# Moving batch 1's kv and query turns behind one more output slot, with a later num 0, reordered w_out casts and one division moved to ScalarE

## The chip, the cores and the metric

One core of one Trainium2 chip. The metric is the device time of one execution, in us. Most executions agree within 0.5%, so ratios are given with their 95% intervals.

## The reference

Linear attention with cosine-weighted features, then a gated feed-forward layer. With r = relu(q) or relu(k), and c, s the cosine and sine of the position:

```python
q_p = concat(r_q * c, r_q * s);  k_p = concat(r_k * c, r_k * s)
kv  = einsum('bhsf,bhsd->bhfd', k_p, v);   z = sum_s(k_p)
x   = (q_p @ kv) / (q_p @ z + 1e-6)          # 8 batches x 8 heads, 576 positions, 64 wide
h   = x @ w_in                               # 4608 x 512 @ 512 x 2048
out = (h * sigmoid(beta * h)) @ w_out        # 2048 x 512, float32
```

## The kernel before

The tokens go through the feed-forward layer in nine chunks of 512. A chunk has 32 slots: 16 of h (four matmuls of 512 columns each), 16 of o (likewise). TensorE runs the slots back to back, and attention work of later batches is woven in between. Chunk 0 is special: batch 1's attention has to be woven into it while the loads of batch 1 and of the weights are still coming in. In the text, a turn is a transpose by TensorE, a take copies it out of PSUM, num 0 and num 1 are the products of q with kv for the two halves of the heads (the prediction's pair 0 and pair 1), and issue time is counted from start to start of the matmuls, since their recorded durations overlap (a matmul of 512 columns at L365 is recorded with 379 ns, and the next one starts 216 ns after it).

```python
def kv_take(jps, bank, eng="dve"):       # copies kv out of PSUM, banks 6 and 7
    ...
def q_turn_pe(b, jp, bank, hold=False):  # nine transposes of q into two banks; take() copies them out
    ...
def second():
    takes.append(q_turn_pe(1, 1, 6, hold=True))     # second query turn, into kv's banks
    cast_out(8)                                     # VectorE, w_out block 8
    takes[0]("act", 0); takes[0]("dve", 1)
    cast_out(9, "a")                                # ScalarE
    takes[0]("dve", 0); takes[0]("act", 1)
    cast_out(10)
    ...                                             # takes[1], blocks 11 to 15

early = {                                           # run behind the slot of that number in chunk 0
    4: lambda: (num_mm(8, 0, 2, 0), num_mm(8, 1, 2, 1), rest()),
    15: lambda: v_scale(1, 1, eng="act"),
    22: lambda: (kv_mm(1, 0, 6), kv_mm(1, 1, 6), kv_take((0, 1), 6, "act"),
                 takes.append(q_turn_pe(1, 0, 4, hold=True))),      # first query turn
    23: second,
    24: lambda: (num_seven(0, 4), x_mul(x_rden(4, 0, 0, 7, (0,)), 0, 7)),   # num 0 and its division
    26: lambda: (num_seven(1, 6), x_mul(x_rden(6, 0, 0, 7, (1,)), 0, 7)),   # num 1 and its division
    28: lambda: x_turn_pe(1, 0, 7, 4, ("act",), (0,)),
    29: lambda: x_turn_pe(1, 0, 7, 5, ("dve",), (1,)),
}
def rest():                                         # loads, in the order of the one load queue
    ...
    load_w("out", 0); load_w("out", 1)
    load_raw(1, "v"); load_raw(1, "k"); load_raw(1, "q")
    x_turn_dma(0, 8, 9)                             # transposing DMA, block 8 of batch 0
    load_w("out", 2, 2); load_w("out", 3, 2)
    ...
```

The lines that the profiles name: L108 casts w_in, L116 (VectorE) and L114 (ScalarE) cast w_out, L189 is a relu on VectorE, L229 a query turn, L234 and L217 take it out, L259 kv, L269 its copy, L280 num, L302 a division, L339 a turn of x, L365 h, L390 o.

## Time and profile before

| | before |
|---|---|
| time, first three runs | 295.02 us (294.88 to 295.82) |
| span of the profiled run | 293.1 us |
| TensorE busy, granted clock | 282.5 us, 0.998 |
| kv of batch 1 starts | 37.98 us |
| q's relu starts (its load has landed) | 39.52 us |
| cast of w_out block 8 starts (likewise) | 41.35 us |
| chunk 1 starts on TensorE | 51.31 us |

The last four rows are starts in the timeline of TensorE and VectorE. The lines of the profile stand in the prediction.

### The profile page before, as it was taken

The numbers are of one execution on the slowest core, as the hardware profiler recorded it, in microseconds if no ns is written. First come the engines' busy times: TensorE is split into PE (matmuls) and PEld (weight loads), VectorE is DVE, ScalarE is ACT, GpSimd is POOL, SyncE is SP. The second block draws the span as 40 slices with busy tenths as digits, with TensorE's granted clock in tenths as the row PEclk, the third lists the DMA queues.
The fourth block names the chain that finished last, engine by engine and source line by source line (L and its number), as shares of the span: only waits on it lengthen the run. The fifth ranks groups of instructions, "written<-read, shape, count | busy, mean of one in ns | idle before, by whom it ended". The sixth has DMA issues, their size and how long they took to land.

```text
span 293.1 us, 7188 instructions
## 1 busy us (share of the span) xinstructions
PE 282.5 (96%) x3046; PEld 143.2 (49%) x3073; DVE 115.0 (39%) x292; ACT 142.5 (49%) x226; POOL 73.3 (25%) x85
## 2 busy tenths in 40 slices
PE   8699989999999999999999999999999999999994
PEld 7454455455445544454445544554455444444444
DVE  5999976743910292029400950087005000000000
ACT  5768756862157324821474137512760277137511
POOL 1440000642381028202640255015701210000000
PEclk9999999999999999999999999999999999999999
DMA  7999999999999079906991699139102910131033
GB/s 259 369 394 382 392 292 389 290 250 341 162 262 352 5 147 236 400 12 130 220 386 58 121 221 394 57 65 188 54 2 53 142 36 0 38 83 24 0 74 72
DMA packets 50737, 53.89 MB, mean 184 GB/s; under 512 B 31233, under 2 KB 31633, under 8 KB 50705
## 3 DMA queue, kind: packets, MB, share of 16 engines
q1 hardware_dynamic: 47744, 45.95, 53.5%
q0 software_dynamic: 2688, 7.34, 10.4%
q8 instruction: 24, 0.39, 0.6%
q10 hardware_dynamic: 272, 0.14, 0.2%
q14 instruction: 9, 0.07, 0.1%
HBM read 36.71 MB, written 9.44 MB: 157 GB/s over the span
## 4 chain that ended last, share of the span: by engine, by line
PE 84%; DMA 8%; DVE 3%; issue 1%; SPq 1%
PE ps L390 39%; PE ps L365 38%; DMA raw_q<-in_q_dram 5%; PE ps L280 3%; DMA raw_v<-in_v_dram 3%; PE ps L259 2%; DVE win L108 2%; PE ps L408 1%; SPq L78 1%; DVE xs L302 1%; PE ps L229 0%; DVE vb L204 0%; DVE rden L295 0%; PE ps L339 0%; DVE qb L189 0%
## 5 line engine op out<-in xcount | busy, mean ns | idle before, releaser
L365 PE MATMUL ps<-xt,win 128*128 128x512 bf16 (+1 forms) x580 | 127.4, 378 | 0.1
L390 PE MATMUL ps<-wout,g_t 128*128 128x512 bf16 x535 | 120.4, 379 | 2.1 <-issue 1.1
L372 ACT ACTIVATE g_t<-ps,beta 128x512 bf16<-128x512 f32 x144 | 98.5, 688 | 33.3 <-PE ps L365 33.3
L365 PEld LDWEIGHTS <-win 128*128 128x128 bf16 x580 | 56.0, 98 | 66.1 <-DVE win L108 0.7
L390 PEld LDWEIGHTS <-g_t 128*128 128x128 bf16 x560 | 53.9, 98 | 63.6
L385 POOL DMA_DIRECT2D out_dram<-o_sb x56 | 37.2, 668 | 144.9 <-ACT o_sb L396 144.9
L396 ACT COPY o_sb<-ps 128x512 f32<-128x512 f32 x35 | 20.2, 587 | 98.2 <-PE ps L390 94.0
L271 DVE CAST kv<-ps 128x520 bf16<-128x520 f32 x6 | 4.2, 699 | 68.3 <-PE ps L259 68.3
L217 POOL TENSOR_TENSOR qs<-qt,tanr 128x1152 bf16<-128x1152 bf16 x12 | 28.4, 2382 | 7.2 <-DMA qt<-qb 6.4
L411 DVE COPY o_sb<-ps 128x256 f32<-128x256 f32 (+1 forms) x2 | 0.7, 358 | 62.9 <-PE ps L408 62.9
L302 DVE TENSOR_TENSOR xs<-ps,rden 128x768 bf16<-128x768 f32 (+5 forms) x27 | 23.1, 862 | 0.9
L291 DVE TENSOR_TENSOR den<-ps,eps 128x12 f32<-128x12 f32 (+4 forms) x26 | 4.2, 160 | 33.6 <-PE ps L280 33.5
L214 DVE TENSOR_SCALAR vb<-raw_v,cos 128x256 bf16<-128x256 f32 x63 | 17.1, 347 | 0.0
L214 DVE TENSOR_SCALAR vb<-raw_v,sin 128x256 bf16<-128x256 f32 x54 | 14.7, 347 | 0.0
L280 PEld LDWEIGHTS <-qt 64*64 64x64 bf16 x576 | 10.5, 106 | 4.7 <-issue 3.4
L280 PE MATMUL ps<-kv,qt 64*64 64x65 bf16 x576 | 11.7, 195 | 0.5 <-ACT kv L269 0.5
L189 DVE TENSOR_SCALAR qb<-raw_q 128x1152 bf16<-128x1152 f32 x16 | 11.4, 752 | 1.6 <-DMA raw_q<-in_q_dram 1.6
L259 PE MATMUL ps<-vb,rk 64*64 64x130 bf16 x576 | 10.2, 218 | 1.7 <-ACT rk L187 1.6
L280 PE MATMUL ps<-kv,qs 64*64 64x65 bf16 x576 | 11.5, 193 | 0.0
L108 DVE CAST win<-w_stage 64x512 bf16<-64x512 f32 x26 | 11.2, 433 | 0.6
L259 PEld LDWEIGHTS <-rk 64*64 64x64 bf16 x576 | 8.5, 106 | 5.6 <-issue 2.5
L189 DVE TENSOR_SCALAR rk<-raw_k 128x2304 bf16<-128x2304 f32 (+2 forms) x9 | 10.5, 1172 | 0.6 <-DMA raw_k<-in_k_dram 0.6
(59 smaller groups left out, 98.5 us busy)
## 6 DMA issues: line engine op xcount, KB each, us to landing
raw_v<-in_v_dram SPq DMA_DIRECT2D x7, 1152.0 KB, 10.5
raw_k<-in_k_dram SPq DMA_DIRECT2D x7, 1152.0 KB, 13.2
raw_q<-in_q_dram SPq DMA_DIRECT2D x7, 1152.0 KB, 7.4
out_dram<-o_sb POOLq DMA_DIRECT2D x56, 128.0 KB, 4.0
w_stage<-in_moe_w_in_dram SPq DMA_DIRECT2D x3, 1024.0 KB, 13.6
w_stage<-in_moe_w_out_dram SPq DMA_DIRECT2D x2, 1024.0 KB, 8.8
w_stage<-in_moe_w_out_dram SPq DMA_DIRECT2D x4, 512.0 KB, 11.2
out_dram<-o_sb SPq DMA_DIRECT2D x14, 128.0 KB, 2.3
```

The source lines that it names most:

```text
L108: nc.vector.tensor_copy(o, a)
L189: nc.vector.tensor_scalar(dst, src, scalar1=0.0, scalar2=None, op0=ALU.max)
L214: nc.vector.tensor_scalar(o, a, scalar1=t[:, n : n + 1], scalar2=None, op0=ALU.mult)
L217: eng.tensor_tensor(dst.rearrange("q n (g p) -> q n g p", g=2), src.rearrange("q n (g p) -> q n g p", g=2), tanr[:, n0:n1].unsqueeze(2).to ...
L259: nc.tensor.matmul(t[jj * HP : (jj + 1) * HP, g], lhsT=rk[hs, n, 2 * jp + jj, :], rhs=vb[hs, n, 2 * jp + jj].rearrange("q s e -> q (s e)") ...
L280: nc.tensor.matmul(ps[cols, bank + jj, slot * E : (slot + 1) * E], lhsT=(qt, qs)[cs][rows, jp, n, cols], rhs=kv[rows, g, jp, cs, :], start ...
L302: nc.vector.tensor_tensor(o.rearrange("q j n s d -> q j (n s) d"), nv[:, :, a:z, :, 0:D].rearrange("q j n s d -> q j (n s) d"), rden[:, :, ...
L365: nc.tensor.matmul(ps[:, h_bank(c, jt), blocks.start * 64 : blocks.stop * 64], lhsT=win[jt // 4][:, mi, (jt % 4) * P : (jt % 4 + 1) * P], ...
L372: nc.scalar.activation(g_t, ps[:, h_bank(c, jt)], AF.Silu, scale=beta[:, jt : jt + 1])
L385: eng.dma_start(out=out_v[bb, n][:, m0:m1], in_=o_sb[hf * HP : (hf + 1) * HP, m0:m1])
L390: nc.tensor.matmul(o_ps, lhsT=gs[c, jt][:, tt * P : (tt + 1) * P], rhs=wout[jt // 4][:, jt % 4, :], start=(jt == 0), stop=(jt == JT - 1))
L396: nc.scalar.copy(o_sb, o_ps)
```

## The change

It means to fill an idle stretch of TensorE ahead of the first query turn with slot 23, whose weights are there long before, and then to keep the rest of the chain from being pushed.

```diff
-    x_mul(x_rden(6, 0, 7, 8, (1,)), 7, 8)              # stood behind the two x_mul
+    x_mul_act(x_rden(6, 0, 7, 8, (1,)), 7)             # now ahead of them
 def second():
+    kv_mm(1, 0, 6); kv_mm(1, 1, 6); kv_take((0, 1), 6, "act")
+    takes.append(q_turn_pe(1, 0, 4, hold=True))
     takes.append(q_turn_pe(1, 1, 6, hold=True))
     ...
-    cast_out(11, "a"); cast_out(12)
-    for j in range(13, JT):
+    for j in (11, 12, 14, 15):
         cast_out(j, "a")
 early = {
-    22: lambda: (kv_mm(1, 0, 6), kv_mm(1, 1, 6), kv_take((0, 1), 6, "act"),
-                 takes.append(q_turn_pe(1, 0, 4, hold=True))),
     23: second,
-    24: lambda: (num_seven(0, 4), x_mul(x_rden(4, 0, 0, 7, (0,)), 0, 7)),
+    25: lambda: (num_seven(0, 4), x_mul(x_rden(4, 0, 0, 7, (0,)), 0, 7), cast_out(13)),
```

More of the change, by code (lines that the diff above doesn't have):

```diff
@@ L534, in second @@
     def second():
+        kv_mm(1, 0, 6)
+        kv_mm(1, 1, 6)
+        kv_take((0, 1), 6, "act")
+        takes.append(q_turn_pe(1, 0, 4, hold=True))
         takes.append(q_turn_pe(1, 1, 6, hold=True))
@@ L545, in second @@
             takes[1](e, i)
-        cast_out(11, "a")
-        cast_out(12)
-        for j in range(13, JT):
+        for j in (11, 12, 14, 15):
             cast_out(j, "a")
```

## The prediction

> **What bounds the kernel now.** I read the totals first, then the chain that ended last, then TensorE's own order of work around the change. The totals say that TensorE is the engine to watch: it is busy 282.5 of 293.1 us, at a granted clock of 0.998.
>
> ```profile
> PE 282.5 (96%) x3046; PEld 143.2 (49%) x3073; DVE 115.0 (39%) x292; ACT 142.5 (49%) x226; POOL 73.3 (25%) x85
> ```
>
> So 10.6 us of the span have no matmul, and only those, and matmuls that could be left out, are to be had. The change leaves out no matmul. The chain of work that ended last, in order of time, shows where the rest is:
>
> ```profile
> 3.02 8.94 DMA raw_v<-in_v_dram
> ...
> 24.08 15.41 DMA raw_q<-in_q_dram
> 39.52 0.77 DVE qb L189
> 41.06 0.81 PE ps L390 x3
> ...
> 52.72 10.47 PE ps L365 x48
> ...
> 82.30 11.22 PE ps L365 x52
> ```
>
> The columns are start, length, and what. From 40.3 us on the chain is TensorE nearly without a break (the waits of TensorE after 53 us sum to 1.0 us in six pieces of up to 0.2, all labelled "issue"). Ahead of that it runs through a load: batch 1's q, issued at 24.08, lands at 39.49, and the relu of its first half (0.77 us) is what TensorE waits for. TensorE in order of time, before the stretch that changes and in it:
>
> ```profile
> 31.84 6.21 PE L390 MATMUL ps<-wout,g_t 128*128 128x512 bf16 x27
> 37.98 1.22 PE L259 MATMUL ps<-vb,rk 64*64 64x130 bf16 x72
> 40.33 0.68 PE L229 MATMUL ps<-ident,qb 128*128 128x128 bf16 x9 [1.13 <-DVE qb L189]
> 41.06 0.81 PE L390 MATMUL ps<-wout,g_t 128*128 128x512 bf16 x3
> 41.71 0.67 PE L229 MATMUL ps<-ident,qb 128*128 128x128 bf16 x9
> 42.21 1.03 PE L390 MATMUL ps<-wout,g_t 128*128 128x512 bf16 x4
> ```
>
> The bracket is idle time and its cause. Slots 16 to 22 of chunk 0 are 28 output matmuls (27 recorded), then kv of batch 1, then 1.13 us of nothing until q's relu is done. Behind it stand the four matmuls of slot 23 (three recorded), which need none of this: their weights were cast long before. This 1.13 us is the prize.
>
> VectorE and ScalarE in the same window say what else could hold TensorE once that gap is filled:
>
> ```profile
> 39.52 1.43 DVE L189 TENSOR_SCALAR qb<-raw_q 128x1152 bf16<-128x1152 f32 x2 [1.58 <-DMA raw_q<-in_q_dram]
> 41.35 0.48 DVE L116 TENSOR_SCALAR wout<-w_stage,rbeta 128x512 bf16<-128x512 f32 x1 [0.40 <-DMA w_stage<-in_moe_w_out_dram]
> 41.75 1.42 DVE L217 TENSOR_TENSOR qs<-ps,tanr 128x512 bf16<-128x512 bf16 x2
> 45.45 0.49 DVE L116 TENSOR_SCALAR wout<-w_stage,rbeta 128x512 bf16<-128x512 f32 x1 [0.56 <-DMA w_stage<-in_moe_w_out_dram]
> 46.33 1.09 DVE L302 TENSOR_TENSOR xs<-ps,rden 128x896 bf16<-128x896 f32 x1
> 47.81 1.09 DVE L302 TENSOR_TENSOR xs<-ps,rden 128x896 bf16<-128x896 f32 x1
> ```
>
> The relus of both halves of q are over only at 40.95. Block 8 of w_out lands at 41.33 and its cast ends at 41.83; slot 24 needs it. Block 12's cast waits 0.56 us for its own load and holds the division of pair 0 up behind it.
>
> [...]the chain's 52 matmuls in 11.22 us are 216 each[...], and four matmuls of a slot are 0.87 us.[...] For two scaled copies of 64 columns[...] the same operation on pair 0 took 0.50 us in the trace, which I use.[...] ScalarE waits four times, 1.6 us in all, for VectorE's qs before its qt.[...]
>
> **Part 1: kv and the query turns behind slot 23.** Nothing is removed; 4 x 216 = 0.87 us of matmuls go ahead of kv. From the trace, slot 22 ends its issue at 37.98, so kv starts at 37.98 + 0.87 = 38.85 (its last input, k's relu, ended at 37.93, so it is no longer even close), and 1.15 us later, its length on the chain in the steady batches, TensorE is free: 40.00. The first query turn still cannot start before 40.33. So the gap falls from about 1.2 us of issue time to 0.33: 0.87 gained at this point. But the next two things now come sooner than their inputs:
> - The first turn issues in 0.50 us (nine loads in 0.50), to 40.83. The second stood behind slot 23 and needed nothing; now it waits for the second half's relu: 40.95 plus 0.05 to wake, 41.00. Loss 0.17. Its bank 6 also waits for kv to be copied out: kv ends about 40.07, the copy takes 0.59 on ScalarE, 40.76; not the last.
> - The second turn issues to 41.50. Slot 24 needs block 8 of w_out, cast until 41.83 at the end of a load that does not move: 41.88. Loss 0.38. Before, slot 24 started at 42.21, so at this point the gain is 0.33.
>
> **Part 2: num 0 a slot on.** Before, num 0 started at 43.22 although slot 24 had issued by 42.21 + 0.87 = 43.08: it waited for the last qs of pair 0 (VectorE, until 43.17). That is 0.14 us. Now slot 25 comes first; slots 24 and 25 take 41.88 to 43.61, past 43.17, so the wait is gone: 0.14 gained. (The 0.16 "issue" gap after num 0 is where slot 25's first matmul is missing from the records; I count nothing for it.) Slot 25 needs block 9's cast on ScalarE, done at 42.13; slot 26 needs block 10, done by VectorE at 43.56, and starts about 44.2. Neither binds. Num 1 then starts about 45.1, after its takes (VectorE to 44.88, ScalarE to 44.77).
>
> **Part 3: w_out casts reordered.** Block 12 goes from VectorE to ScalarE, block 13 to VectorE behind the division of pair 0. ScalarE: block 11 to 45.39, block 12 from its landing at 45.41 to 46.17; slot 28 needs it at about 46.5. VectorE: the division of pair 0 starts at 44.90 instead of 45.85, takes 1.57 as before, ends 46.45; block 13 to 46.87 (slot 29 needs it at 47.8); the division of pair 1 ends about 48.4, and its turn stands at 48.6. This part gains nothing by itself; it keeps num 0's later place from pushing the second turn of x.
>
> From 41.88 on TensorE's work is eight slots, 32 x 216 = 6.92, two nums at 0.60 together 1.20, two x turns at 0.39: 8.90. Sum 50.78, against a chunk 1 that began at 51.31. **Gain 0.53 us**: 0.33 + 0.14, and 0.06 of rounding.
>
> **Part 4: block 7 of pair 1 on ScalarE.** VectorE loses a 0.29 us multiply but does this block's denominators first, so the seven other blocks' two multiplies end at about 18.5, not 18.23. The last transpose, now bound by these, goes from 18.88 to about 18.7, and VectorE's w_in casts begin 0.3 us sooner. ScalarE is idle from 17.0 to 18.26, so two copies (0.50) fit there. TensorE is some 0.2 us earlier through chunk 0's first half. But it meets a load: q lands at 39.49 whatever the engines do, since the DMA engines moved 385 to 395 GB/s in every window I asked for from 14 to 32 us and were still above 350 in the mean from 32 to 38; no earlier issue makes that shorter. The 0.2 us are handed back as a longer wait ahead of the first query turn. **Worth nothing** at the end.
>
> **Rivals.**
> - *The gap is gained whole.* 0.87 + 0.14, perhaps 0.2 more from part 4: 294.0 or just under. For it: TensorE bounds everything after, and moves over unhindered. Against: the relu at 40.95 and the cast at 41.83 are fixed by loads, and I see no way around the latter.
> - *The wait only moves.* Slot 24's weights, then VectorE's run from takes to divisions, hold TensorE until the old times: 295.0. For: VectorE is in the same order until 44.88, and the second division ends (48.4) only some 0.2 us before its turn. Against: before, the second turn of x had nothing to wait for at 49.19, with its division over at 48.90.
> - *A transfer shifts.* The stretch from 38 to 40 us has only 145 GB/s, while a transposing DMA and the rest of q land; if a little earlier work on VectorE changes the order in which the queue is fed, q or w_out could land half a microsecond sooner or later: 293.9 or 295.4. In the trace nothing on the queue of these loads hangs on what the change moves, so I give it little.
>
> **Range and chances.** 295.02 - 0.53 = 294.5. The three runs before lay from 294.88 to 295.82, so the spread of runs is as large as the gain. First rival and last set the low end, 293.9; the second and a slow median set the high end, 295.1. Two per cent is 5.9 us, eleven times the whole gap that can be filled and over half of all idle time of TensorE; neither side of 2% is reachable without a fault that I don't see.
>
> **What would show it.** Right: kv starts at about 38.85; the idle ahead of the first query turn falls from 1.13 to about 0.3; short new idles ahead of the second turn (q's relu) and slot 24 (a w_out cast); no wait ahead of num 0; chunk 1 begins about 50.8; identical lengths after it. Wrong: slot 24 starting before 41.8 or after 42.1 (the cast of block 8 is then not what binds); an idle ahead of the second x turn (VectorE's run binds); q landing elsewhere than 39.5 (the loads moved); part 4 seen in the start of chunk 1.

0.33 + 0.14 and 0.06 of rounding are 0.53 us, 295.02 - 0.53 is 294.5 us, and each length is one of the trace before (216 ns a matmul, from 52 in 11.22 us; "0.05 to wake": q's first relu ends at 40.27 us, the turn that waits for it starts at 40.33). In the trace the w_out casts on ScalarE have a median of 722 ns, and the division of one block of one pair (part 4's multiply) takes 0.29 us.

## The result, and the profile after

294.55 us (294.51 to 294.71, four runs) against 295.12 (294.88 to 295.82, four runs). The ratio is 0.9978, interval 0.996 to 0.9995; it is the mean time of one kernel's fast runs over that of the other's of the same rounds, so not quite the ratio of the medians. The predicted 294.5 was hit. Two later sessions on two chips, with six runs of the changed kernel in each, did not confirm the gain: 0.9997 and 0.9999 (below). So the number was right in its session, and the reason has to be looked at.

The totals after, from the page; TensorE has no matmul more or less:

```profile
PE 282.4 (96%) x3046; PEld 142.5 (49%) x3073; DVE 114.3 (39%) x291; ACT 142.6 (49%) x228; POOL 73.3 (25%) x85
```

The chain that ended last, after (start, length, what). It now hangs on w_in and w_out loads, no longer on q's; 45.31 shows a stop inside num 1 that nothing explains there:

```profile
6.29 12.66 DMA w_stage<-in_moe_w_in_dram
...
31.17 9.53 DMA w_stage<-in_moe_w_out_dram
...
41.22 0.65 PE ps L229 x9
...
45.13 0.18 PE ps L280 x6
45.31 0.14 issue
45.45 0.60 PE ps L280 x45
```

TensorE in order of time, after:

```profile
31.91 7.07 PE L390 MATMUL ps<-wout,g_t 128*128 128x512 bf16 x31
38.91 1.22 PE L259 MATMUL ps<-vb,rk 64*64 64x130 bf16 x72
40.06 0.68 PE L229 MATMUL ps<-ident,qb 128*128 128x128 bf16 x9
41.20 0.66 PE L229 MATMUL ps<-ident,qb 128*128 128x128 bf16 x9 [0.46 <-DVE wout L116]
41.70 1.89 PE L390 MATMUL ps<-wout,g_t 128*128 128x512 bf16 x7
```

kv starts at 38.91, as predicted, and the first turn follows without idle: the 1.13 us are gone. But the second turn now idles 0.46 us. The profile names a cast as the cause. A cast of weights is no input of a query turn, so the name is only that of the semaphore event that came last; in the second trace of this kernel the same wait is put down to the copy of kv (`<-ACT kv L269`), which empties the turn's bank. VectorE after:

```profile
38.89 1.43 DVE L189 TENSOR_SCALAR qb<-raw_q 128x1152 bf16<-128x1152 f32 x2 [1.63 <-DMA raw_q<-in_q_dram]
40.72 0.49 DVE L116 TENSOR_SCALAR wout<-w_stage,rbeta 128x512 bf16<-128x512 f32 x1 [0.40 <-DMA w_stage<-in_moe_w_out_dram]
41.12 1.48 DVE L217 TENSOR_TENSOR qs<-ps,tanr 128x512 bf16<-128x512 bf16 x2
...
44.71 1.09 DVE L302 TENSOR_TENSOR xs<-ps,rden 128x896 bf16<-128x896 f32 x1
45.72 0.48 DVE L116 TENSOR_SCALAR wout<-w_stage,rbeta 128x512 bf16<-128x512 f32 x1
...
46.66 1.09 DVE L302 TENSOR_TENSOR xs<-ps,rden 128x896 bf16<-128x896 f32 x1
```

Both loads came 0.63 us sooner than in the trace before (38.89 against 39.52, and 40.72 against 41.35), although the prediction held that nothing moves them. And ScalarE's copy of kv, before and then after:

```profile
39.31 0.59 ACT L269 CAST kv<-ps 128x520 bf16<-128x520 f32 x1 [1.98 <-PE ps L259]
```

```profile
40.56 0.59 ACT L269 CAST kv<-ps 128x520 bf16<-128x520 f32 x1 [3.89 <-PE ps L229]
```

Before, the copy starts 0.11 us after kv's last matmul (37.98 + 1.22 = 39.20). After, 0.43 us (38.91 + 1.22 = 40.13). The records of semaphore events have kv's at 40.16; ScalarE's wait instruction was over at 40.19; the copy that stands behind it started at 40.56 with nothing to wait for. So three questions: is the earlier landing the change's doing, what holds the copy of kv, and what is the change worth without both.

### The profile page after: what moved, and what is told of

It is laid out like the page before. It is cut to its first block, busy times and chain, and to the rows that moved or that the text cites. A ratio compares the mean times of both kernels' runs of the same rounds, so it can differ in the third digit from the quotient of the medians.

```text
span 292.9 us, 7188 instructions
## 1 busy us (share of the span) xinstructions
PE 282.4 (96%) x3046; PEld 142.5 (49%) x3073; DVE 114.3 (39%) x291; ACT 142.6 (49%) x228; POOL 73.3 (25%) x85
## 4 chain that ended last, share of the span: by engine, by line
PE 84%; DMA 9%; DVE 4%; issue 1%; SPq 0%
PE ps L390 39%; PE ps L365 38%; DMA w_stage<-in_moe_w_in_dram 4%; PE ps L280 3%; DVE win L108 3%; DMA w_stage<-in_moe_w_out_dram 3%; PE ps L259 2%; DMA raw_q<-in_q_dram 2%; PE ps L408 1%; DVE wout L116 0%; PE ps L339 0%; PE ps L229 0%; SPq L78 0%; DVE xs L302 0%; DVE o_sb L411 0%
## 5 line engine op out<-in xcount | busy, mean ns | idle before, releaser
L302 DVE TENSOR_TENSOR xs<-ps,rden 128x768 bf16<-128x768 f32 (+4 forms) x26 | 22.8, 884 | 1.0 <-DVE rden L295 0.2
L280 PEld LDWEIGHTS <-qs 64*64 64x64 bf16 x576 | 10.5, 105 | 0.2 <-issue 0.2
```

The costliest lines, as they stand in the source:

```text
L280: nc.tensor.matmul(ps[cols, bank + jj, slot * E : (slot + 1) * E], lhsT=(qt, qs)[cs][rows, jp, n, cols], rhs=kv[rows, g, jp, cs, :], start ...
L302: nc.vector.tensor_tensor(o.rearrange("q j n s d -> q j (n s) d"), nv[:, :, a:z, :, 0:D].rearrange("q j n s d -> q j (n s) d"), rden[:, :, ...
```

## The experiments

Each ran with a profile and, beside the kernel before on the same chip, for three or five rounds. All give correct results.

**First call: chance in the loads, and block 7 by itself.** The first two kernels are the two of the study, unchanged. `block7_only` is the kernel before with the first hunk of the diff alone, `block7_undone` the changed kernel without it.

```diff
 # block7_only: kernel before; block7_undone: changed kernel with - and + exchanged
+    x_mul_act(x_rden(6, 0, 7, 8, (1,)), 7)
     x_mul(got, 0, 4)
     x_mul(got, 4, 7)
-    x_mul(x_rden(6, 0, 7, 8, (1,)), 7, 8)
```

> The kernel before, unchanged: a second trace, to see how far the loads' landings vary by themselves. In the first trace batch 1's q landed at 39.49 us, in the trace after the change at 38.87, although the DMA engines had moved the same bytes by 22 and by 36 us. Theory A, the landing varies by chance[...]: q lands somewhere from 38.8 to 39.6 here, and the kernel takes 295.0. Theory B, the change moves the landing: 39.5 again here and in every run that leaves the change's first part out, 38.9 in every run that has it.

> The changed kernel, unchanged. Expected ratio to before 0.998, 294.5 us. ScalarE's copy of kv waits some 0.36 us after its semaphore was met in the first trace (wait over at 40.19, copy from 40.56). If that is bound to the instruction's place in ScalarE's stream, it is there again with the same size; if it was chance, it is gone and the second query turn starts about 0.3 us sooner after kv.

> The kernel before with block 7 of pair 1 on ScalarE and nothing else of the change. The prediction's step: worth nothing, 295.0, ratio 1.000 with 0.999 to 1.001, since q's landing takes the 0.2 us back. Rival: the loads are fed sooner (theory B) and the first query turn starts 0.6 us sooner: 294.4.

> The changed kernel with block 7 back on VectorE. ScalarE then has two instructions fewer ahead of the copy of kv. Prediction's step (worth nothing): 294.5, as the changed kernel. Theory of the place in the stream: the 0.36 us ahead of the copy of kv are gone, the copy starts under 0.1 us after its semaphore, the second turn follows the first with 0.1 us less idle or more, and the kernel is 0.1 to 0.4 us faster than the changed one: 294.2. Theory B of the loads: q lands at 39.5 and it is 0.1 slower.

Measured, median and ratio: before again 295.16 (0.9999), after again 294.98 (0.9997, interval 0.9978 to 1.0017), block7_only 295.24 (0.9997), block7_undone 295.34 (1.0011, 0.9987 to 1.0034). No time differs beyond its interval, and neither the 294.5 us expected of the changed kernel nor the 294.2 of block7_undone came. The traces do differ.

The landing of q varies from run to run. q's relu started at 39.52 in the first trace before and at 39.04 in the second; with block 7 on ScalarE at 38.89 and 38.95 (the changed kernel) and 39.47 (`block7_only`); with the change but without block 7 at 40.01. That is theory A; theory B (the change moves the landing) asked for two groups. The parts of one load land apart as well: in the first trace before, k's sixteen parts landed from 34.10 to 36.55 us. Over all eleven traces with the old load order q's relu started anywhere from 38.89 to 40.05. So comparing two single traces mixes the change with this. Part of the spread goes with how late the queue was fed. In six of the eleven, q's load was issued at 23.89 to 24.15 us and its last part landed at 38.87 to 39.49; in the other five, issued at 24.31 to 24.99, it landed at 39.45 to 40.03. What makes the landings differ at the same time of issue stays open.

The 0.36 us ahead of the copy of kv are not chance. They are 0.36 us in all three traces that have block 7's two instructions on ScalarE and 0.04 in all three that have not, also in the otherwise changed kernel, `block7_undone`. Its TensorE:

```profile
39.33 1.22 PE L259 MATMUL ps<-vb,rk 64*64 64x130 bf16 x72
40.82 1.34 PE L229 MATMUL ps<-ident,qb 128*128 128x128 bf16 x18 [0.28 <-DVE qb L189]
42.38 1.89 PE L390 MATMUL ps<-wout,g_t 128*128 128x512 bf16 x7 [0.21 <-DVE wout L116]
```

Both turns are one group here (x18), 0.28 us idle for q's relu ahead and 0.21 us behind for the cast of block 8: two of the waits that the prediction had named, in a run with a late load. The third stands inside the group, where the line doesn't show it: the second turn starts 0.21 us after the start of the first's last transpose, against 0.06 where nothing holds it (kv_at_22), so it waits 0.16 us for the relu of q's second half.

**The remaining parts, the place of the copy, and kv back at its slot.**

```diff
 # kv_at_22: changed kernel
-    kv_mm(1, 0, 6); kv_mm(1, 1, 6); kv_take((0, 1), 6, "act")     # out of second()
+    22: lambda: (kv_mm(1, 0, 6), kv_mm(1, 1, 6), kv_take((0, 1), 6, "act")),
 # act_shift: changed kernel
-    15: lambda: v_scale(1, 1, eng="act"),
+    15: lambda: (nc.scalar.copy(warm, zero_b), v_scale(1, 1, eng="act")),
 # num0_at_24: changed kernel
-    25: lambda: (num_seven(0, 4), x_mul(...), cast_out(13)),
+    24: lambda: (num_seven(0, 4), x_mul(...), cast_out(13)),
 # casts_old: changed kernel
-    for j in (11, 12, 14, 15): cast_out(j, "a")                   # and no cast_out(13) at slot 25
+    cast_out(11, "a"); cast_out(12)
+    for j in range(13, JT): cast_out(j, "a")
```

> The changed kernel with kv and its copy back behind slot 22; both query turns stay together behind slot 23. In the two traces of the changed kernel the second turn waits 0.47 us for the copy of kv, which empties its bank. Theory: with slot 23 (0.87 us) between kv and the turns this wait is gone; the second turn follows the first without idle, or waits for q's relu alone, and slot 24 starts when block 8's cast is over (landing of that w_out block + about 0.55 us). Slot 24 to start 0.4 us sooner than in the changed kernel at the same landings (41.2 to 41.3 where block 8 lands at 40.7), and the run to take 0.3 to 0.5 us less: ratio to before 0.9965 to 0.9985. Rival: VectorE's takes and divisions hold TensorE later on, and nothing is gained over the changed kernel.

> The changed kernel with one idle copy of one column added to ScalarE ahead of the scaling of batch 1's v, so that the copy of kv is the 65th and not the 64th of its recorded instructions. Theory of the place: the 0.36 us between met semaphore and copy are gone (under 0.1 us), the second turn starts 0.3 us sooner after kv, if q's relu is over by then. Rival (the copy waits for the transposes' writes, or for their semaphore): 0.36 us again. Worth 0.1 to 0.3 us at most.

> The changed kernel with num 0 back behind slot 24 (its place before), the casts as changed. Prediction's step: a wait of TensorE for the last qs of pair 0 ahead of num 0. With slot 24 at 41.6 and the qs over at 42.5 the wait is about 0.1 us by the traces; by the prediction 0.14 and more, since slot 24 comes sooner. So slower than the changed kernel by 0.1 to 0.3 us, or nothing where slot 24 came late. Rival: num 0 sooner makes the division sooner and something later gains: not slower.

> The changed kernel with the w_out casts in their old order (block 12 on VectorE ahead of the division of pair 0, 13 to 15 on ScalarE). Prediction's step: worth nothing by itself, but block 12's load then holds up the divisions: the first ends about 47.4 at a landing of 45.4, the second 1.5 us later, against x turns wanted at 47.4 and 48.7. So an idle of 0 to 0.3 us ahead of an x turn, and as much in the time; at the earlier landings of the last traces nothing.

Measured: kv_at_22 294.98 (0.999, 0.9971 to 1.0008), act_shift 295.24 (1.0, 0.9981 to 1.002), num0_at_24 295.21 (1.0007, 0.9988 to 1.0025), casts_old 294.74 (0.9991, 0.9972 to 1.0009). Again the times alone decide nothing; kv_at_22's lies above the range expected for it (0.9965 to 0.9985).

*act_shift.* TensorE, then ScalarE's copy:

```profile
39.20 1.22 PE L259 MATMUL ps<-vb,rk 64*64 64x130 bf16 x72
40.45 1.38 PE L229 MATMUL ps<-ident,qb 128*128 128x128 bf16 x18
42.48 1.89 PE L390 MATMUL ps<-wout,g_t 128*128 128x512 bf16 x8 [0.66 <-DVE wout L116]
```

```profile
40.52 0.59 ACT L269 CAST kv<-ps 128x520 bf16<-128x520 f32 x1 [3.06 <-PE ps L259]
```

The copy starts 0.10 us after kv (39.20 + 1.22 = 40.42), though the transposes follow as closely as before. So neither the transposes' writes nor their semaphore held it. One more or two fewer instructions ahead of it do away with the 0.36 us: the cost belongs to the place, the 64th recorded instruction of ScalarE (its waits counted). The second turn's wait shrinks with it but isn't gone: the x18 hides 0.20 us of it (0.26 us from the first turn's last start to the second's first, against 0.06), as the copy of kv ends at 41.11 and the relu of q's second half at 41.06. This run's w_out load was late (the cast began at 41.94), and slot 24 waited 0.66 us for it, so the time shows no gain.

*num0_at_24.* The wait ahead of num 0 is back, with 0.31 us where 0.1 to 0.3 was expected:

```profile
41.87 1.02 PE L390 MATMUL ps<-wout,g_t 128*128 128x512 bf16 x4
...
43.20 0.22 PE L280 MATMUL ps<-kv,qt 64*64 64x65 bf16 x4 [0.31 <-DVE qs L217]
```

Yet chunk 1 starts 13.13 us after slot 22's end, against 13.05 and 13.09 in the first two traces of the changed kernel: the stop inside num 1 (below) isn't there, and the one pays for the other (from slot 24 to chunk 1 it is 9.42 us here and 9.39 in the first trace of the changed kernel).

*casts_old.* Block 12's cast waits 0.60 us for its load on VectorE and pushes the second division to 48.61, but the turn of x that needs it starts at 49.01, without idle:

```profile
45.16 0.49 DVE L116 TENSOR_SCALAR wout<-w_stage,rbeta 128x512 bf16<-128x512 f32 x1 [0.60 <-DMA w_stage<-in_moe_w_out_dram]
...
47.52 1.09 DVE L302 TENSOR_TENSOR xs<-ps,rden 128x896 bf16<-128x896 f32 x1
```

```profile
49.01 0.55 PE L339 MATMUL ps<-ident,xs 128*128 128x128 bf16 x7
```

Chunk 1 starts 13.06 us after slot 22's end, as with the new order. The casts' order is worth nothing at this landing.

*kv_at_22.* kv, slot 23, both turns and slot 24 run without idle, although the copy of kv has its 0.38 us here too; it has slot 23's length to hide in:

```profile
39.23 1.22 PE L259 MATMUL ps<-vb,rk 64*64 64x130 bf16 x72
40.38 1.04 PE L390 MATMUL ps<-wout,g_t 128*128 128x512 bf16 x4
41.25 1.17 PE L229 MATMUL ps<-ident,qb 128*128 128x128 bf16 x18
42.26 1.89 PE L390 MATMUL ps<-wout,g_t 128*128 128x512 bf16 x8
```

Chunk 1 starts 12.08 us after slot 22's end. Of the 13.07 us of the changed kernel, 0.64 are the second turn's wait in issue time (from 40.06 + 0.50 to 41.20 in the first trace) and 0.35 the stop inside num 1; 12.08 + 0.64 + 0.35 = 13.07.

**The transposing DMA in the load queue, and the best version.** In the trace before, the window from 38 to 40 us, in which q ends and the transposing DMA runs, moved little. The line gives packets and mean rate:

```profile
DMA packets 213, 0.29 MB, mean 145 GB/s; under 512 B 83, under 2 KB 83, under 8 KB 213
```

```diff
 # before_turn8: kernel before; kv22_turn8: kv_at_22
-        x_turn_dma(0, 8, 9)                              # in rest()
+    9: lambda: x_turn_pe(0, 8, 9, 1, ("act",)),          # in early
```

> The kernel before, but block 8 of batch 0 is turned by TensorE behind slot 9 (two transposes, a copy of 256 columns by ScalarE) and not by a transposing DMA, which stood in the load queue between batch 1's q and w_out's third quarter. So far chunk 1 of the kernel before began 11.58 us after q's landing in both its load-bound traces, and q's sixteen parts all landed within 0.1 us, about 1.8 us behind the last bytes of the steady stream. Theory: the loads drain at that transposing DMA, and without it q lands 1 us or more sooner (about 38.0) and block 8 of w_out 1.5 us sooner; TensorE then waits for neither, chunk 1 begins 12.4 us after slot 22's end, some 0.3 to 1.0 us sooner than in the kernel before: ratio 0.997 to 0.999. Rival: q[...] lands near 39.3 as before; only w_out comes 0.46 us sooner, and the time is the same.

> The changed kernel with kv behind slot 22 and block 8 of batch 0 turned by TensorE, as the best that the runs point to. If the transposing DMA drains the loads: no wait of TensorE from slot 22 to chunk 1, which begins 12.3 us after slot 22's end whatever the landings; 294.2, ratio 0.996 to 0.998, and its runs spread less. Rival: q at 39.3; then no better than the run with kv behind slot 22 (0.999).

> The changed kernel a third time, to be timed on the same chip beside the two others. From its traces chunk 1 begins 13.1 to 13.2 us after slot 22's end, or 9.4 us after the landing of w_out's block 8, whichever is later; the kernel before needs 12.3 or 9.8. So about 0.35 us better where the load is late and up to 0.9 worse where it is early: near 1.000 in the mean, 0.998 to 1.001.

> The best version once more, on another chip. Its five runs took 294.01 in the median against 295.33, ratio 0.9953; but its trace, set against the kernel before at the same landings (chunk 1 of that begins 11.6 us after q's landing, so at 50.6 against 49.98), accounts for 0.6 us alone, 0.998. If its lead comes from the waits that it no longer has, the ratio lies between 0.996 and 0.998 here, and its interval stays under 1; if the first lead was luck with the loads of those runs, it is 0.998 to 1.000.

Measured: before_turn8 295.5 (1.0002, 0.9986 to 1.0019); kv22_turn8 294.01 (293.58 to 294.21), ratio **0.9953** (0.9935 to 0.997), and on another chip 293.95 (293.71 to 294.64), **0.9971** (0.9957 to 0.9985); after_third 295.37 (0.9999, 0.9983 to 1.0015).

The rival was right on q's landing. The same window of before_turn8 is full:

```profile
DMA packets 406, 0.78 MB, mean 388 GB/s; under 512 B 30, under 2 KB 30, under 8 KB 406
```

But q's relu starts at 39.94 there and the first turn waits 1.19 us. In the traces of both orders q's last part lands 2.9 to 3.0 us after k's last part, with or without the transposing DMA: so the DMA does not set that distance; what does was not shown. What the DMA cost was behind q: block 8's load now lands 1.37 us after q's instead of 1.82. The kernel before does not wait for that block, so it gains nothing. kv22_turn8 needs the block sooner, and has no wait left in its first trace:

```profile
38.12 1.22 PE L259 MATMUL ps<-vb,rk 64*64 64x130 bf16 x72
39.26 1.04 PE L390 MATMUL ps<-wout,g_t 128*128 128x512 bf16 x4
40.14 1.17 PE L229 MATMUL ps<-ident,qb 128*128 128x128 bf16 x18
41.14 1.89 PE L390 MATMUL ps<-wout,g_t 128*128 128x512 bf16 x8
...
50.19 1.03 PE L365 MATMUL ps<-xt,win 128*128 128x512 bf16 x4
```

In its second trace q's relu came at 39.40, and the two turns lost 0.3 us to it (chunk 1 starts 12.36 us after slot 22's end, against 12.08).

**All traces by one rule.** A is the end of slot 22's issue (kv's start, less 0.87 where slot 23 stands ahead of it), R the start of q's relu, B the start of chunk 1. In the three traces in which the kernel before's order waits for q, B - R is 11.79, 11.76 and 11.75. In block7_only, which has that order too and came late to kv (A is 39.71, against 37.90 to 39.23 elsewhere), B - A is 12.19. So the old order's B is the later of R + 11.77 and A + 12.19, and each other trace can be set against what the old order would have made of its loads (worked out, not measured):

| run | A | R | B, old order | B measured | difference |
|---|---|---|---|---|---|
| changed, first trace | 38.04 | 38.89 | 50.66 | 51.09 | +0.43 |
| after_again | 37.90 | 38.95 | 50.72 | 51.00 | +0.28 |
| after_third | 39.01 | 40.05 | 51.82 | 51.86 | +0.04 |
| casts_old | 38.07 | 39.19 | 50.96 | 51.12 | +0.16 |
| num0_at_24 | 38.16 | 39.51 | 51.28 | 51.29 | +0.01 |
| act_shift | 38.33 | 39.63 | 51.40 | 51.53 | +0.13 |
| block7_undone | 38.46 | 40.01 | 51.78 | 51.44 | -0.34 |
| kv_at_22 | 39.23 | 39.87 | 51.64 | 51.31 | -0.33 |
| kv22_turn8 | 38.12 | 39.05 | 50.82 | 50.19 | -0.63 |
| kv22_turn8_again | 38.09 | 39.40 | 51.17 | 50.45 | -0.72 |

The changed kernel is at A + 12.85 to 13.09. Its variants in which block 8's load comes last are 9.6 us after that cast's begin (act_shift 9.59, block7_undone 9.61, kv_at_22 9.61). So it beats the old order where q's relu starts more than 1.3 us after slot 22's end (13.05 - 11.77; in the trace before it was 1.54), and loses where it starts sooner (0.85 to 1.05 in its own three traces). By this working the versions with kv at slot 22 are better in all three of their traces, by 0.33 to 0.72 us, at q's relu 0.64 to 1.31 us after slot 22's end.

**The stop inside num 1.** In five traces TensorE's loads of num 1 stop at the same instruction, num 1's seventh load of weights, with 0.12 to 0.39 us from one load to the next. A 16 KB packet of the queue that the profile names `q8 instruction` (24 packets, 0.39 MB) ends 1.36 to 1.57 us before the stop is over in each of them; in the trace of the changed kernel it runs from 42.83 to 43.94, and the loads resume at 45.45. In the nine without the stop TensorE reaches the place 1.49 to 2.74 us after that packet, so the two ranges overlap a little. No run was made that moves the place on TensorE: what causes the stop, and whether it hangs on that packet, was not shown.

## Why the prediction was right or wrong

- **The time, 294.5 against 294.55: right in its session, and half luck.** With the landings of the trace before (A 37.98, cast of block 8 at 41.35) the changed kernel's rules give the later of 37.98 + 13.05 = 51.03 and 41.35 + 9.61 = 50.96, against 51.31: 0.28 us and not the 0.53 predicted. Over all three sessions its ratios are 0.9978, 0.9997 and 0.9999.
- **kv at 38.85, the gap filled: right** (38.91; no idle ahead of the first turn).
- **The step that failed** is "Its bank 6 also waits for kv to be copied out: kv ends about 40.07, the copy takes 0.59 on ScalarE, 40.76; not the last." It was the last. kv ended at 40.13, the copy at 40.56 + 0.59 = 41.15. Predicted loss at the second turn 0.17, measured 0.64 in the same issue time. 0.36 of it is the place of the copy in ScalarE's stream, which the block 7 part brought about (act_shift, without it, still waits 0.20); the rest fits q's earlier load, which let the first turn stand right behind kv (40.06 and not 40.33).
- **Slot 24 bound by block 8's cast: right where the load is late** (act_shift 0.66 us idle, block7_undone 0.21), not in the first trace after, where the second turn came last.
- **Part 2, num 0: right about the wait.** There is none in the changed kernel and 0.31 us with it undone, against 0.14. That it is worth as much at chunk 1 is not shown (13.13 against 13.05 and 13.09 us).
- **Part 3, nothing by itself: right at the landing of its one trace** (13.06 against 13.05 and 13.09 us).
- **Part 4: nothing at the end, right by the time, incomplete in kind.** VectorE was free 0.4 us sooner (18.44 against 18.82) but then waited 0.54 us for w_in's second quarter, so its casts began later, at 18.98 against 18.84. TensorE was 0.22 us ahead behind the last turn of x (18.73 against 18.95), as predicted, and level again by the first output slot (31.91 against 31.84). But the two instructions moved the copy of kv onto the costly place.
- **From slot 24 to chunk 1, 8.90 us: too short.** 41.70 to 51.09 are 9.39. Without the stop inside num 1 they are 9.05 (kv_at_22, kv22_turn8), so 0.34 are the stop and 0.15 were missing from the sum.
- **"q lands at 39.49 whatever the engines do": wrong that it stands still.** It wanders by 1.2 us. The rival of a shifting transfer was set aside as a thing the change might do; it happens with either kernel unchanged (39.52 and 39.04 before, 38.89, 38.95 and 40.05 after). Its ground, that nothing on this queue hangs on what the change moves, was misread too: in the trace before, the second of the w_out loads ahead of v, k and q is issued right behind VectorE's casts of w_in (22.39), which part 4 moves. In the first trace after, q was issued at 24.04 against 24.08, so that didn't bring the 0.63 us.
- **The lengths of single instructions in the trace before: they held.** In the changed kernel's trace a w_out cast on ScalarE has a median of 721 ns against 722, VectorE's division of 896 columns takes 1.09 us in both, and the matmuls of a slot follow each other by 216 ns, as in the 52 that took 11.22 us in the trace before.
- **A slip in the range:** 5.9 us is eleven times the predicted gain of 0.53, not "the whole gap that can be filled" (1.13 us, five times). Nothing hangs on it.

What stays open: kv22_turn8 is 1.3 and 1.0 us ahead by its medians, and the table accounts for 0.6 to 0.7. The granted clock doesn't explain the rest: with only those runs of the kernel before that had 0.998 or more, the lead on the first chip is still 1.29 us by the means. It may be that its runs met good loads, or that runs of the old order meet late ones oftener than the profiled ones did; one or two profiles per kernel can't tell. How much of the lead is the turn on TensorE and how much kv's place is open too: kv_at_22 (0.999) and kv22_turn8 ran in different sessions.

## What to carry to other kernels

When a gap ahead of a load is filled with independent work, list everything that the filled stretch used to hide: here a copy that empties a bank had 1.8 us of slack (over at 39.90, needed at 41.71) and ended with none. Separate the work that needs the load (the query turns) from the work that doesn't (kv and its copy), and move only the former. And before a gain of a quarter of a per cent is read from two traces, take the same kernel's trace again: the loads alone moved the start of chunk 1 by half a microsecond (51.31 and 50.80 us in the two traces of the kernel before).

## What else the traces show

- The copy of kv as ScalarE's 64th recorded instruction, behind a wait of its own, started 0.36 to 0.38 us after that wait in each trace with it there, and 0.04 us after it in the three that have it two places sooner. Stops of 0.32 us show at ScalarE's 192nd (before) and 320th (after) as well, so these three places lie 128 apart; an 8 KB packet of the profile's queue `q14 instruction` begins 1.1 to 3.3 us after each of the three. That the first hangs on the place is shown by the runs that move it; what makes the place cost, and whether the packets have to do with it, is not.
- The parts of a load drift apart: 2.45 us between the first and the last part of one 1.15 MB load (34.10 to 36.55, k in the trace before), with 1.2 us of spread in the next load's landing from run to run.
- The transposing DMA cost the plain load queued behind it 0.45 us (1.82 us from q's landing to the next block's with it, 1.37 us without, in before_turn8).
